# Fused attention, mixture of experts and a last layer on one core: the second pair's bias from SBUF, softplus' sums, gate's and conversion's steps in other places, expert 0's scaling on GpSimd

## The chip, the core and the metric

The kernel runs on one core of a Trainium2 chip. A core has a matrix engine (TensorE), a vector engine (VectorE), a scalar engine (ScalarE, ACT), a general one (GpSimd) and a queue engine (SyncE, SP), each with an instruction stream of its own that runs in order; semaphores tie them together. They work on SBUF, an on-chip memory of 128 partitions; TensorE writes into PSUM, a small memory of eight banks per partition. The metric is the device time of one execution in microseconds.

## What is computed

```python
# attention: q, k, v are (2, 8, 576, 64), s is (2, 8, 576)
scores = q @ k.T / sqrt(64)
cum = cumsum(maximum(s, 0))
scores = where(causal, -1e9, scores + minimum(-(cum[:, None] - cum[None, :]), 0))
x = softmax(scores) @ v                      # -> (1152, 512)
# mixture: w_gate (512, 8), w1 (8, 512, 1024), w2 (8, 1024, 512)
P = exp(x @ w_gate - max)
for _ in range(8):
    P /= P.sum(1, keepdims=True) + 1e-9
    P /= P.sum(0, keepdims=True) + 1e-9
    P *= 1152 / 8
x = sum(P[:, e:e+1] * (maximum(x @ w1[e], 0) @ w2[e]) for e in range(8))
# last layer: w_in (512, 2048) and w_out (2048, 512), given as float64
h = x @ w_in
out = (maximum(h, 0) + log1p(exp(-abs(h)))) @ w_out
```

## The kernel before

All is written under a manual schedule: the order of the Python statements is the order of each engine's instructions, and waits follow from the data.

**Precision.** TensorE multiplies in a reduced float32 type, so every operand is split into a high part (a copy on ACT) and a low part (a subtraction on VectorE or GpSimd), and each product is three matmuls (high x high, low x high, high x low). In names, `xh`, `xl` are the two parts of the activations, `w1h`, `w1l`, `w2h`, `w2l` those of the weights, `hh`, `hl` those of the hidden layer.

**Attention** (until about 121 us) goes over 8 pairs of heads, each in 5 blocks of queries; such a block is a unit. The units are pipelined by hand: in pass n, the letters of "YSKAXVWBTED" do one stage each of different units. The causal bias is brought into the scores as a product of its own: `init_bias` (L436) fills the tiles `bq`, `bk`, `be` of a pair with zeros and ones, and `load_bias` (L444) puts two rows of the cumulative sums per head into them. The sums `cs` lie in SBUF with one row per head (L467 scales s, L469 scans, L474 and L475 split); L477 copies them to DRAM as `c8d`. There are two sets of tiles: set 0 for pair 0 is filled from `cs`, all others from `c8d`. SP issues nearly all transfers in program order: q and k by `load_qk` (L418), the first weights of the mixture, `raw` (L134), bias (L449, L454). GpSimd sums and differences of the first weights (L154, `sums1`) and the scaling of the probabilities by their row sums (L618) stand in one stream. TensorE transposes the probabilities (`tr`, L630) and multiplies them by v (`pv`, L662, L672); ACT copies the transposed ones out of PSUM (`pt`, L650). In the last four pairs of batch 0 and 1, `build` makes the seven combinations of activations that the mixture's products need, one `yield` at a time, two per unit (L82 sums, L85 high, L88 low parts).

**Mixture.** Sixteen half-experts x = 0 to 15 (two per expert, XE = 2). A half-expert's first layer is four quarters of work, done by a scheme of seven products per quarter (`Unit.p1` to `p7`, each six 128x288 matmuls at L286), its second layer is `downs` (three 128x512 matmuls at L371 for each of nine tiles of tokens and four slices of the hidden layer, a yield after each three). `total` adds the finished tile to `acc`: for x < 2 without a gate (L383), then with the factor of the gate (L388), and for x = 2 expert 0's sum is first scaled by its gate (L387). `play` runs strings such as A_SEQ and B_SEQ: a1 to b7 are products, d three matmuls of downs, `=0` to `=2` and `w0` to `w3` put a generator that prepares the next weights in a queue, `back`. After each product or d, `step` moves that queue by one, every sixth time the gate's steps (`gate_steps`, x = 0 and 1), and later every third time the conversion of the last layer's float64 weights to float32 (`convert`, from x = 2; 32 items of seven steps; items come by `fetch`). What an eviction still has to do is put off with `defer(k, ...)` and done k flushes later; products and downs flush once or twice each.

**Switch and last layer.** When x = 15 is done, `turn` transposes the result (L901, L911) back into activations, batch 0 and then 1. The last layer, x = 16 to 19, uses `plain` products (12 matmuls at L350). Its eviction is softplus: three ACT functions (L249 abs, L250 exp, L251 ln), then `sums` (L255 on VectorE, L256 on GpSimd, L257 on VectorE), `high` (L260 VectorE, L261 ACT) and `rest_` (L264 VectorE), over four sets of tiles.

## Time and profile before

| | us |
|---|---|
| runs, median (lowest to highest, 3 runs) | 1129.07 (1127.46 to 1132.74) |
| profiled execution, its own time | 1129.13 |
| its span | 1127.4 |
| TensorE busy | 1085.5 (96%) |
| VectorE busy | 750.0 (67%) |
| ScalarE busy | 525.8 (47%) |
| GpSimd busy | 358.7 (32%) |
| share of the chain that ended last: TensorE / VectorE / ScalarE | 80% / 8% / 5% |

The span is the time from the first to the last instruction in the profile; 1.7 us of the execution lie around it. In a timeline row stand the start, the duration, engine, line, operation and the tile written and read; in brackets how long the engine stood idle before it and what ended that. "x4" are four instructions of one kind in a row. The granted clock is TensorE's, as a share of 2.4 GHz.

### The profile page before, as it was taken

The page shows a single profiled execution, that of the slowest core. Times are in us where ns is not written, and L with a number is a line of the kernel's source. Part 1 is how long each engine was busy: PE and PEld are TensorE (multiplying, and loading weights), DVE is VectorE, ACT ScalarE, POOL GpSimd, SP SyncE. Part 2 cuts the span into 40 slices and gives each one's busy share as a digit, 9 for nine tenths or more (in the row PEclk, how much of TensorE's full clock was granted, in tenths as well). Part 3 has the DMA queues.
Part 4 walks back from the last instruction along what each step waited for, and adds up shares of the span by engine and source line. Part 5 has one row for each costly group of instructions (what it writes and reads, how often), then busy time and mean ns, then how long its engine had stood idle before and what let it go on. Part 6 is the DMA issues. An engine that isn't in the chain of part 4 may idle for free.

```text
span 1127.4 us, 18117 instructions
## 1 busy us (share of the span) xinstructions
PE 1085.5 (96%) x6692; PEld 952.9 (85%) x6692; DVE 750.0 (67%) x1705; ACT 525.8 (47%) x1246; POOL 358.7 (32%) x429
## 2 busy tenths in 40 slices
PE   5989899999999999999999999999999999999998
PEld 4767888797889888888888888988889888888886
DVE  4555537749878787787787777864555576666664
ACT  4988644234334344344343433433334276655552
POOL 8775411112314144141431414322020032323231
PEclk8998999999999999999999999999999999999999
DMA  5222102031322223222232222311112111111002
GB/s 190 71 71 66 39 1 72 4 111 48 113 94 94 94 77 126 88 94 94 94 111 87 94 94 94 103 50 45 38 38 76 38 38 38 38 38 38 1 1 84
DMA packets 30424, 78.48 MB, mean 70 GB/s; under 512 B 6048, under 2 KB 10656, under 8 KB 30336
## 3 DMA queue, kind: packets, MB, share of 16 engines
q1 hardware_dynamic: 27768, 68.93, 18.8%
q0 software_dynamic: 2560, 8.39, 2.0%
q8 instruction: 52, 0.85, 0.3%
q14 instruction: 36, 0.29, 0.1%
q10 hardware_dynamic: 8, 0.01, 0.0%
HBM read 66.02 MB, written 10.82 MB: 68 GB/s over the span
## 4 chain that ended last, share of the span: by engine, by line
PE 80%; DVE 8%; ACT 5%; issue 3%; POOL 3%; DMA 1%; SPq 0%; POOLq 0%; ACTq 0%; DVEq 0%
PE py L371 40%; PE ph L286 30%; PE ph L350 3%; PE sc L550 2%; POOL a L256 1%; DVE a L260 1%; PE pv L662 1%; ACT a L250 1%; ACT a L249 1%; PE tr L636 1%; DVE a L255 1%; ACT eb L605 1%; DVE acc L383 1%; PE tr L630 1%; DVE a L257 1%
## 5 line engine op out<-in xcount | busy, mean ns | idle before, releaser
L371 PE MATMUL py<-w2h,hh 128*128 128x512 f32 x720 | 287.2, 399 | 10.7 <-DVE acc L383 6.3
L371 PE MATMUL py<-w2h,hl 128*128 128x512 f32 x720 | 285.0, 396 | 0.0
L371 PE MATMUL py<-w2l,hh 128*128 128x512 f32 x720 | 284.9, 396 | 0.0
L286 PE MATMUL ph<-xh,w1h 128*128 128x288 f32 x896 | 265.9, 297 | 0.4 <-ACT v L294 0.3
L286 PE MATMUL ph<-xh,w1l 128*128 128x288 f32 x896 | 265.6, 296 | 0.0
L286 PE MATMUL ph<-xl,w1h 128*128 128x288 f32 x896 | 264.2, 295 | 0.0
L286 PEld LDWEIGHTS ph<-xh,w1h 128*128 128x128 f32 x896 | 168.9, 188 | 18.3 <-ACT v L294 1.5
L286 PEld LDWEIGHTS ph<-xl,w1h 128*128 128x128 f32 x896 | 169.2, 189 | 16.6
L286 PEld LDWEIGHTS ph<-xh,w1l 128*128 128x128 f32 x896 | 169.1, 189 | 0.0
L371 PEld LDWEIGHTS py<-w2h,hl 128*128 128x128 f32 x720 | 135.4, 188 | 32.6 <-DVE hl L237 0.2
L371 PEld LDWEIGHTS py<-w2h,hh 128*128 128x128 f32 x720 | 135.4, 188 | 26.6 <-DVE acc L383 8.9
L234 ACT ACTIVATE hh<-ph 128x288 fp32r<-128x288 f32 x192 | 78.4, 410 | 154.7 <-DVE ph L336 85.3
L371 PEld LDWEIGHTS py<-w2l,hh 128*128 128x128 f32 x720 | 135.5, 188 | 11.4
L200 POOL TENSOR_TENSOR w2l<-raw,w2h 128x512 fp32r<-128x512 f32 x40 | 54.1, 1352 | 260.0 <-ACT w2h L198 259.9
L388 DVE SCALAR_TENSOR_TENSOR acc<-py,gate,acc 128x512 f32<-128x512 f32 x126 | 93.8, 745 | 58.2 <-PE py L371 57.2
L294 ACT ACTIVATE v<-ph 128x288 f32<-128x288 f32 x128 | 50.9, 411 | 168.7 <-PE ph L286 160.4
L888 POOL TENSOR_TENSOR cm<-cm,ct 128x512 f32<-128x512 f32 x32 | 45.1, 1409 | 222.4 <-DVE ct L886 222.4
L237 DVE SCALAR_TENSOR_TENSOR hl<-ph,hh 128x288 fp32r<-128x288 f32 x192 | 86.2, 452 | 32.2 <-ACT hh L234 30.1
L256 POOL TENSOR_TENSOR a<-a,a 128x288 f32<-128x288 f32 x64 | 51.8, 809 | 160.1 <-DVE a L255 159.8
L148 DVE TENSOR_TENSOR w1l<-raw,w1h 128x512 fp32r<-128x512 f32 (+1 forms) x144 | 94.3, 655 | 9.8 <-ACT w1h L145 9.5
L145 ACT ACTIVATE w1h<-raw 128x512 fp32r<-128x512 f32 (+1 forms) x144 | 83.0, 576 | 1.6 <-PE ph L286 1.6
L350 PE MATMUL ph<-xh,w1h 128*128 128x288 f32 x256 | 76.0, 297 | 0.8 <-ACT xh L912 0.8
(176 smaller groups left out, 1683.1 us busy)
## 6 DMA issues: line engine op xcount, KB each, us to landing
raw<-in_w SPq DMA_DIRECT2D x64, 512.0 KB
f<-in_w_in SPq DMA_DIRECT2D x16, 512.0 KB
f<-in_w_out SPq DMA_DIRECT2D x16, 512.0 KB
wd<-cm POOLq DMA_DIRECT2D x32, 256.0 KB, 2.6
raw<-wd SPq DMA_DIRECT2D x16, 512.0 KB
out<-acc SPq DMA_DIRECT2D x9, 256.0 KB
vv<-in_v SPq DMA_DIRECT2D x8, 256.0 KB
qk<-in_k SPq DMA_DIRECT2D x7, 288.0 KB
```

The source lines that it names most:

```text
L145: nc.scalar.activation(out=hi[:, o], in_=t[:, src], func=AF.Copy)
L148: nc.vector.tensor_tensor(out=lo[:, o], in0=t[:, src], in1=f(hi[:, o]), op=ALU.subtract)
L200: (nc.gpsimd if i else nc.vector).tensor_tensor(out=lo, in0=t[:, r], in1=f(hi), op=ALU.subtract)
L234: nc.scalar.activation(out=hh, in_=z, func=AF.Relu)
L237: nc.vector.scalar_tensor_tensor(out=hl, in0=z, scalar=0.0, in1=f(hh), op0=ALU.max, op1=ALU.subtract)
L256: nc.gpsimd.tensor_tensor(out=a2, in0=a1, in1=a2, op=ALU.subtract)
L286: nc.tensor.matmul(o, u, v, start=(start and c == 0 and n == 0), stop=(c == 1 and n == 2), skip_group_check=True)
L294: nc.scalar.activation(out=t, in_=self.a, func=AF.Copy)
L350: nc.tensor.matmul(o, u, v, start=(n == 0), stop=(n == 11))
L371: nc.tensor.matmul(py[t], u, v, start=(k == 0 and n == 0), stop=(k == NF - 1 and n == 2))
L388: nc.vector.scalar_tensor_tensor(out=a, in0=py, scalar=gate_t[0][:, t, e:e + 1], in1=a, op0=ALU.mult, op1=ALU.add)
L888: nc.gpsimd.tensor_tensor(out=m, in0=m, in1=f(t), op=ALU.add)
```

## The change

1. **Bias.** `init_bias(1)` runs on VectorE, ahead of the scaling of s; it ran on GpSimd, after the other memsets. The bias of pair 1 comes from `cs` in SBUF and is issued once, behind `split_ends(0)`; it came from `c8d` in DRAM, behind the weights. The write of `c8d` stands behind it.
2. **Build.** Two more yields, that is one unit, between the last sum and `high_(2)`.
3. **Softplus.** `sums` are put off by one flush more, `high` and `rest_` by two; the add of the two sums goes from VectorE to GpSimd.
4. **Expert 0's scaling** goes from `total` on VectorE to the start of a group of downs on GpSimd.
5. **Gate.** A step may come after three (first six steps) or seven others, at least three after an a2 or b2, and not between w0 and the next "=".
6. **Conversion.** Four yields between the first two fetches and the first item.
7. **Switch and end.** The products between downs stand behind them, with one more behind w3 (in the diff the string); the last half's last two tiles are groups of their own.

```diff
--- before.py
+++ after.py
@@ -108,7 +108,8 @@
         sum_(2, nc.gpsimd)
-        yield
+        for _ in range(3):
+            yield
         high_(2)
@@ -253,19 +254,19 @@
             nc.vector.tensor_scalar(a2, a1, 1.0, -1.0, ALU.add, ALU.add)
+            nc.vector.scalar_tensor_tensor(out=a3, in0=z, scalar=0.0, in1=a3, op0=ALU.max, op1=ALU.add)
             nc.gpsimd.tensor_tensor(out=a2, in0=a1, in1=a2, op=ALU.subtract)
-            nc.vector.scalar_tensor_tensor(out=a3, in0=z, scalar=0.0, in1=a3, op0=ALU.max, op1=ALU.add)
+            nc.gpsimd.tensor_tensor(out=a3, in0=a3, in1=a2, op=ALU.add)
...
         def high():
-            nc.vector.tensor_tensor(out=a3, in0=a3, in1=a2, op=ALU.add)
             nc.scalar.activation(out=hh, in_=a3, func=AF.Copy)
...
-        defer(0, sums)
-        defer(2, high)
-        defer(3, rest_)
+        defer(1, sums)
+        defer(4, high)
+        defer(5, rest_)
@@ -362,6 +363,10 @@
                 py[t] = ps.tile([P, DM], F32, tag=f"y{1 + nd[0] % 2}", name="py", bufs=1)
+            if x == XE:
+                for t in tiles:
+                    a = acc[0][:, t, :]
+                    nc.gpsimd.tensor_scalar(a, a, gate_t[0][:, t, 0:1], 1.0, ALU.mult, ALU.mult)
             for k, ft in enumerate((0, 2, 1, 3)):
@@ -383,8 +388,6 @@
             e = x // XE
-            if x == XE:
-                nc.vector.tensor_scalar(a, a, gate_t[0][:, t, 0:1], None, ALU.mult)
             nc.vector.scalar_tensor_tensor(out=a, in0=py, scalar=gate_t[0][:, t, e:e + 1], in1=a,
@@ -433,24 +436,24 @@
-            def init_bias(x):
+            def init_bias(x, engine):
                 for t in (bq_t[x], bk_t[x], be_t[x]):
-                    nc.gpsimd.memset(f(t), 0.0)
+                    engine.memset(f(t), 0.0)
                 for j in range(2):
...
                                          (be_t[x], slice(j * REM, (j + 1) * REM), 1.0)):
-                        nc.gpsimd.memset(f(t[j * D:j * D + 4, cols]), one)
+                        engine.memset(f(t[j * D:j * D + 4, cols]), one)
...
                     h = 2 * p + j
-                    x = c8d[h] if p > 0 else f(cs[h:h + 1])
+                    x = c8d[h] if p > 1 else f(cs[h:h + 1])
                     for t, r, cols in ((bk_t, 2, slice(0, S)), (bq_t, 0, slice(0, S))):
...
                     h = 2 * p + j
-                    x = c8d[h, :, NB * P:] if p > 0 else f(cs[h:h + 1, :, NB * P:])
+                    x = c8d[h, :, NB * P:] if p > 1 else f(cs[h:h + 1, :, NB * P:])
                     nc.sync.dma_start(out=f(be_t[p % BB][j * D:j * D + 2, j * REM:(j + 1) * REM]), in_=x)
@@ -464,17 +467,17 @@
             nc.vector.memset(ones, 1.0)
+            init_bias(1, nc.vector)
             nc.vector.tensor_scalar(s_sb, s_sb, 0.0, 8.0, ALU.max, ALU.mult)
...
                 nc.vector.tensor_tensor_scan(c8[:, a:b], one_row[:, a:b], s_sb[:, a:b], first, ALU.mult, ALU.add)
-            init_bias(0)
+            init_bias(0, nc.gpsimd)
             cs = ac.tile([B * H, 2, S], F32R, name="cs")
...
             load_bias(0)
-            nc.sync.dma_start(out=c8d, in_=f(cs))
             make_identity(nc, ident)
@@ -494,8 +497,6 @@
                 nc.gpsimd.memset(f(y), 0.0)
-            for x in range(1, BB):
-                init_bias(x)
@@ -554,6 +555,8 @@
             split_ends(0)
+            load_bias(1)
+            nc.sync.dma_start(out=c8d, in_=f(cs))
             load_qk(4)
@@ -764,7 +767,8 @@
                     if i == 1 and p + 1 < B * NP:
-                        load_bias(p + 1)
+                        if p > 0:
+                            load_bias(p + 1)
                         load_v(p + 1)
@@ -861,6 +865,8 @@
             fetch(1)
+            for _ in range(4):
+                yield
             for i, (_, dst) in enumerate(todo):
@@ -917,14 +923,20 @@
         back = []
-        tick = [0]
-
-        def step():
+        tick = [0, 0, 0, 0]
+        dense = [False]
+        def step(z=""):
...
             tick[0] += 1
+            tick[1] += 1
+            tick[2] = 0 if z[1:] == "2" else tick[2] + 1
             if x < XE:
-                if tick[0] % 6 == 0:
+                if tick[1] >= (3 if tick[3] < 6 else 7) and tick[2] > 2 and not dense[0]:
                     next(gates, None)
+                    tick[1] = 0
+                    tick[3] += 1
             elif x < NX - 2 and tick[0] % 3 == 0:
@@ -957,6 +969,8 @@
             for z in seq.split():
+                if z[0] in "=w":
+                    dense[0] = z[0] == "w"
                 if z[0] == "=":
@@ -967,7 +981,7 @@
                     todo[z]()
-                step()
+                step(z)
@@ -988,7 +1002,7 @@
             play(A_SEQ if x < NX else A_PLAIN, products(x, 1), downs(x, A_GROUPS))
-            d = downs(x, B_GROUPS)
+            d = downs(x, B_GROUPS if x + 1 < NH else [(t,) for t in range(NB, NTT)])
             if x + 1 < NX:
@@ -1000,7 +1014,7 @@
                 u = products(NX, 0)
-                play("p d d w0 p d d w2 p d d w1 p d d w3", u, d)
+                play("d d w0 p d d w2 p d d w1 p d d w3 p", u, d)
                 back.append(turn(1))
...
```

Line numbers move by one to three in these parts (L449 is now L452, L134 is L135, L249 is L250). How the instructions then stand is shown at three places.

SP, at the start: `bk_94`, `bq_92`, `be_96` are the tiles of set 1, `raw` the first weights. Before, from the write of c8d on:

```order
L477 DMA c8d<-cs 16x1152
L523 DMA endf<-in_q 64x64 x2
L418 DMA qk<-in_k 128x576
L418 DMA qk<-in_q 128x576
L134 DMA raw_181<-in_w 128x1024
L134 DMA raw_183<-in_w 128x1024
L134 DMA raw_185<-in_w 128x1024
L134 DMA raw_187<-in_w 128x1024
L449 DMA bk_94<-c8d 2x576
```

and now, from the third of the four rows for set 1 on:

```order
L452 DMA bk_94<-cs 2x1x576
L452 DMA bq_92<-cs 2x1x576
L457 DMA be_96<-cs 2x1x64 x2
L559 DMA c8d<-cs 16x1152
L421 DMA qk<-in_k 128x576
L421 DMA qk<-in_q 128x576
L135 DMA raw_187<-in_w 128x1024
```

The six pieces for set 1 stand ahead of c8d's write, k, q and the weights; they stood behind all of them.

ScalarE, at the end of attention: `xh_75` are the combinations of batch 1, `pt` the copies of the last but one unit's probabilities. Before:

```order
L85 ACTIVATE xh_75<-xr 128x2x288
L650 ACTIVATE pt<-tr 128x512 x2
L85 ACTIVATE xh_75<-xt 128x4x288
L650 ACTIVATE pt<-tr 128x512
L650 ACTIVATE pt<-tr_1791 64x128
L721 ACTIVATE xr<-pv 128x512
L721 ACTIVATE xr<-pv_1805 128x64
```

and now:

```order
L85 ACTIVATE xh_75<-xr 128x2x288
L653 ACTIVATE pt<-tr 128x512 x3
L653 ACTIVATE pt<-tr_1791 64x128
L85 ACTIVATE xh_75<-xt 128x4x288
L724 ACTIVATE xr<-pv 128x512
L724 ACTIVATE xr<-pv_1805 128x64
L85 ACTIVATE xh_75<-xr 128x288
```

The copy of the combined tile xt stands behind the last copies of pt instead of between them.

ScalarE, in the last layer (L249 to L251 are the three functions, L261 the high part; the number of `a` tells the product apart). Before:

```order
L249 ACTIVATE a_10585<-ph 128x288
L250 ACTIVATE a_10585<-a_10585 128x288
L251 ACTIVATE a_10587<-a_10585 128x288
L261 ACTIVATE hh<-a_10587 128x288
L249 ACTIVATE a_10618<-ph 128x288
L250 ACTIVATE a_10618<-a_10618 128x288
L251 ACTIVATE a_10620<-a_10618 128x288
```

and now (L250 to L252 and L262):

```order
L250 ACTIVATE a_10583<-ph 128x288
L251 ACTIVATE a_10583<-a_10583 128x288
L252 ACTIVATE a_10585<-a_10583 128x288
L262 ACTIVATE hh<-a_10554 128x288
L250 ACTIVATE a_10616<-ph 128x288
L251 ACTIVATE a_10616<-a_10616 128x288
L252 ACTIVATE a_10618<-a_10616 128x288
L262 ACTIVATE hh<-a_10585 128x288
```

L261 stood right behind its own product's functions; L262 stands behind those of the next product.

## Rows read from the trace of the kernel before

**Rows 1.** Page, part 1: busy time, share of the span and instructions of each engine.

```profile
PE 1085.5 (96%) x6692; PEld 952.9 (85%) x6692; DVE 750.0 (67%) x1705; ACT 525.8 (47%) x1246; POOL 358.7 (32%) x429
```

**Rows 2.** Windows: us of stretch, busy per engine, granted clock, DMA share.

```profile
122.00:125.40 3.40, 3.40 (x17) 3.28 (x18) 3.15 (x6) 2.15 (x4) 0.81 (x1) 0.50 0.00 0
200.50:203.90 3.40, 3.40 (x13) 2.90 (x12) 2.10 (x9) 0.77 (x2) 0.90 (x2) 0.50 0.02 5
339.00:386.50 47.50, 47.50 (x278) 42.58 (x277) 37.84 (x74) 18.73 (x43) 15.34 (x16) 1.00 0.28 95
912.00:926.00 14.00, 12.17 (x87) 10.78 (x85) 12.43 (x27) 11.90 (x29) 5.32 (x6) 1.00 0.23 77
977.00:1024.50 47.50, 45.73 (x270) 40.74 (x269) 31.70 (x71) 27.75 (x66) 13.43 (x16) 1.00 0.15 45
```

**Rows 3.** TensorE's waits: awaited instruction; us in total, times, longest.

```profile
PE py L371 <- DVE acc L383: 6.3, 6, 1.5
...
PE py L371 <- DVE acc L388: 3.4, 2, 2.5
PE pcs L830 <- DVE hl L237: 3.1, 1, 3.1
PE sc L550 <- DMA bq<-cs: 2.8, 1, 2.8
PE pv L672 <- ACT pt L650: 1.9, 1, 1.9
```

**Rows 4.** SP's timeline, start: start, us, issue, pieces [idle before <-releaser].

```profile
7.49 1.21 SPq L454 DMA_DIRECT2D be<-cs  x2
...
11.65 1.85 SPq L134 DMA_DIRECT2D raw<-in_w  x4
```

**Rows 5.** VectorE's timeline, start of the kernel.

```profile
0.91 0.54 DVE L464 MEMSET one_row<- 16x576 f32 x1 [0.91 <-PEq L1049]
...
2.54 0.77 DVE L467 TENSOR_SCALAR s_sb<-s_sb 16x576 f32<-16x576 f32 x1 [0.95 <-DMA s_sb<-in_s]
```

**Rows 6.** Timelines of GpSimd, then TensorE, pair 0, units 0 and 1.

```profile
17.07 0.73 POOL L154 TENSOR_TENSOR raw<-raw 128x256 f32<-128x256 f32 x1 [1.64 <-DMA raw<-in_w]
17.77 0.94 POOL L618 TENSOR_SCALAR eb<-eb,st 128x256 f32<-128x256 f32 x2
...
20.15 0.82 PE L550 MATMUL sc<-bk,bq 64*128 64x128 f32 x2 [3.91 <-DMA bq<-c8d]
20.90 1.11 PE L630 MATMUL tr<-ident,eb 128*128 128x128 f32 x4
```

**Rows 7.** ScalarE's timeline, end of attention.

```profile
119.58 1.16 ACT L85 ACTIVATE xh<-xt 128x1152 fp32r<-128x1152 f32 x1 [1.97 <-POOL xt L82]
```

**Rows 8.** VectorE's timeline in the gate, x = 1.

```profile
195.11 0.23 DVE L837 TENSOR_REDUCE gs<-gate 128x9 f32<-128x72 f32 x1
...
197.31 0.45 DVE L237 SCALAR_TENSOR_TENSOR hl<-ph,hh 128x288 fp32r<-128x288 f32 x1
```

**Rows 9.** VectorE's timeline, first item of the conversion.

```profile
253.65 0.43 DVE L870 TENSOR_SCALAR f<-f 128x512 f32<-128x512 f32 x1 [5.96 <-DMA f<-in_w_in]
```

**Rows 10.** The chain that ended last, in the last layer: start, us, what.

```profile
1002.98 0.93 PE py L371 x4
1003.91 1.59 PE ph L350 x12
...
1008.65 0.40 ACT a L249
...
1010.01 0.82 POOL a L256
1010.85 0.47 DVE a L260
...
1011.69 0.41 ACT a L249
```

**Rows 11.** VectorE's timeline, switch, second set of transposes.

```profile
919.58 0.98 DVE L264 TENSOR_TENSOR hl<-a,hh 128x288 fp32r<-128x288 f32 x1
```

## The prediction

> **What bounds the kernel now.** I began with the page. TensorE is busy for 96% of the span [rows 1], so at most some 42 us are open, and its own matmuls are not changed. Then a table of windows: a whole steady half-expert has TensorE busy for 47.50 of 47.50 us [rows 2], and in the listing of TensorE's waits no large entry falls there. So work that the change moves in the steady part is worth nothing; what can move lies in stages where TensorE idles: the start of attention, its end, the gate, the start of the conversion, the switch and the last layer. The waits [rows 3] name them. Last I read, for each, the engine TensorE waited for and what stood ahead of the awaited instruction there. The windows also show what an idle stretch costs behind itself: after the gate's long wait and after the end of attention the granted clock is 0.50 (the lower level, 1.2 GHz) for 3.40 us each [rows 2], about 1.7 us of lost work each time.
>
> The profiled execution took 1129.13 us, its span is 1127.4 us, and the median of the runs is 1129.07; the sum is made against 1129.13, so against the median as well.
>
> **Start: the second pair's bias.** Nine memsets go to VectorE ahead of the scaling of s. Six have 576 columns; the one of that length took 0.54 us, and with three short ones that is about 3.5 us. VectorE sat idle there for 0.95 us until s had landed at 2.54 [rows 5]. It was free at about 1.6 (the memset at 0.91 and a short one), so it gets to the scaling near 5.0 instead of 2.54: 2.5 us later. No other work hides that: TensorE's first scores wait 2.8 us for this very bias [rows 3]. All of pair 0 moves by 2.5.
> SP then issues the second bias from SBUF (six pieces, 0.6 us each by the pair that took 1.21: 3.6 us) ahead of the four weight loads, which so far began at 11.65 [rows 4]. Now they begin near 11.65 + 2.5 + 3.6 = 17.75. The first weight's sum on GpSimd started 17.07, that is 5.4 us after the first issue, after a wait of 1.64 us for the load [rows 6]; it would start at about 23.2. In GpSimd's order it stands ahead of the scaling of unit 1, whose transposes TensorE started at 20.90. Sum 0.73 plus half of the scaling's 0.94: the transposes start near 24.4, so 3.5 us later. What goes is the wait of 3.91 us for the bias [rows 6]: the bias itself lands near 16.7, before TensorE asks for it at about 18.2. So a wait for the weights takes the place of the wait for the bias. The loads have less beside them now and may land sooner, so I take **-3.0**. GpSimd loses the nine memsets, and c8d's write moves behind the second bias; the first to need either is the third pair's bias, many units later, so both count nothing. Its ends: -5, when the memsets and GpSimd's collide as well, and +1.4, when the weights are in time.
>
> **End of attention: the build is two units later.** ACT's conversion of xt waited 1.97 us for GpSimd's sum and then took 1.16 [rows 7]; the copies of pt stand behind it, and TensorE waited 1.90 for those [rows 3]. Afterwards the copies stand ahead of it. The gain is not 1.9, since the last quick build follows on ACT and limits TensorE's third product next: with half clock granted there anyway [rows 2], that product comes 1.7 us earlier by my count. I take **+1.7** (0.5 to 3.4, the upper end with the half clock gone). In the middle of attention the same sums slow GpSimd and VectorE beside it; **+0.5** (-1 to +3).
>
> **Gate.** Each step of the normalisation is a chain on VectorE: from 195.11 seven small operations ran to 197.3, and the eviction hl stood behind them [rows 8]. TensorE waited 3.1 us for such an hl [rows 3] and lost 1.7 by the clock behind that [rows 2]. Smaller gaps at six places from 140 to 215 us add some 2.5 by the starts of the matmuls. That is 7.3 us. The new rule keeps the steps out of the stretch that begins with w0, where VectorE also makes w2's low parts, and runs the first six steps sooner, so that all still fit in the same two half-experts. VectorE remains full in the first part of x=1, where three or four steps now fall; I leave 1.3 us of waits there: **+6.0** (3.5 to 7.5).
>
> **Conversion's start and expert 0's scaling.** VectorE stood still for 5.96 us until the first item landed, its first step being in its queue already [rows 9]; behind it queued evictions and the totals, and TensorE waited 3.4 us in two places for L388 [rows 3]. Four more yields put the first step 12 play steps (some 9 us at this pace) behind the fetch, longer than the landing took. Nine scalings leave VectorE too; on GpSimd they start with their group. One of 512 columns costs there at most 512/288 of the 0.81 us that L256 takes [rows 10], 1.4 us, and four steps of the group, over 2 us of matmuls, lie ahead of the total that reads it. So I cost them at nothing; were GpSimd late, each of nine totals would wait up to 1 us. The gaps of this stage are 4.7 us with restarts and small ones; I leave 0.7: **+4.0** (2.5 to 5).
>
> **Switch.** From 912 to 926 us TensorE is busy 12.17 of 14 [rows 2], since products and transposes alternate faster than ACT and VectorE serve them. Two more products behind the last transpose, and the deferral, spread this. I take **+1.2** (0 to 2.5).
>
> **Last layer: softplus' ring.** This is the part the change touches most. In the chain, ACT's first function of a product (1008.65) is followed by steps on ACT and VectorE, GpSimd's L256 (0.82 us at 1010.01), VectorE's L260 (1010.85), ACT's L261, and only then by the next product's first function at 1011.69 [rows 10]: one turn of the ring is 3.04 us. TensorE needs 12 matmuls, 1.59 us, and six of the downs at 0.93/4 each [rows 10], 2.99 in all, so the ring is a little slower, and the totals that stand behind it on VectorE come late: TensorE waits for L383 six times, 6.3 us [rows 3], with restarts and one wait for ACT's first total about 7.7. After the change ACT reaches L261 two or three flushes after its input is due, so the turn no longer closes through GpSimd. GpSimd has 2 x 0.82 = 1.64 us of work in each 2.99. The split of the last pair into single groups takes away one of the six waits.
> A price stands against that. VectorE's L264 (both operands in SBUF) took 0.98 us beside GpSimd in the switch [rows 11], while L260, of the same form, took 0.47 alone [rows 10]; so GpSimd's second add can hold VectorE up. VectorE is busy for 31.70 of 47.5 us [rows 2], 2.00 a product; without L260 1.53. If nothing meets, the gain is 7.7. If every microsecond of the adds stopped it, 1.53 + 1.64 = 3.17 against 2.99: 64 products x 0.18 = 11.5 lost, against 7.7. I take **+6.0** (-4 to 8), near the upper end, because in the turn of rows 10 L256 ran beside L257 alone, which reads PSUM and took no longer for it.
> The Trainium skill, page "SBUF — State Buffer", section "SBUF: two separate sides", says that VectorE and GpSimd share one port pair under an exclusive lock, so that the later of two such operations stands still for the whole of the other. Rows 11 agree for L264. By it every VectorE operation of this form that meets the two adds would wait for their ends, and the term would be -4; without it 7.7.
>
> **The sum.** -3.0 + 1.7 + 0.5 + 6.0 + 4.0 + 1.2 + 6.0 = 16.4 us. 1129.13 - 16.4 = 1112.7; I say 1112 us, since the gaps left over were each rounded up.
>
> **Rivals.**
> 1. *The weights are in time at the start.* For it: only 1.64 us of wait before, and the bias's transfers no longer lie beside theirs. Against it: SP issues them 6 us later [rows 4]. Then unit 1 starts near 19.5 rather than 20.90; +1.4 and not -3.0, with less idle time before the half clock: about 1107. Chance 0.12.
> 2. *The last layer keeps its waits.* VectorE, held up by the adds, reaches L383 as late as before. For it: rows 11. Against it: nothing waits for the adds within two flushes any more. The 6 us stay: 1118. Chance 0.15.
> 3. *The gate's steps still hold up evictions* in x=1, as they come closer together at first. For it: each is over 2 us of VectorE [rows 8]; against: from the seventh on, six other play steps lie between two of them. About 5 us stay: 1117. Chance 0.10.
> 4. *Slower: GpSimd becomes a lock on VectorE in all of the last layer.* If both adds of each product stop it for their whole length, and half of the 1.0 us per product that it now idles (15.8 of 47.5 us [rows 2]) stays, its product costs 1.53 + 1.64 + 0.5 = 3.67 us. It decides from 2.99 on: 64 products x 0.68 = 43.5 us, and the 6 us aren't gained: 1161. For it: rows 11; against: L256 met L264 only in the switch, and the deferral lets VectorE fill its idle time. Chance 0.03. The skill's lock, named above, is the rule that would bring this about.
> 5. *All terms at their low ends.* -5 + 0.5 - 1 + 3.5 + 2.5 + 0 - 4 = -3.5: about 1132.6. The order moves, but other instructions keep the engines late. Chance 0.05.
>
> **How the numbers follow.** The forecast has the remaining 0.55; its own spread, from the ends of single terms taken apart, is some 7 us either way. The range 1102 to 1122 takes in the forecast's spread, rivals 1, 2 and 3, and leaves out 4, 5 and a share of the forecast's tails, about 2 in 10. A measurement of this kernel can tell about 0.5%, 5.6 us, from no change: faster means below 1123.5, slower above 1134.7. Forecast and rivals 1 to 3 are faster nearly throughout (0.92, less 0.02 of tails), rival 5 is the same, rival 4 slower.
>
> **What would show it.** Start: the scaling of s near 5.0, the first weight load near 17.6, unit 1's transposes near 24, waiting by way of GpSimd for a weight and not for bq. Gate: no pcs or pg wait over 1 us and no half clock near 200. Conversion: VectorE not idle for 6 us near 247, no L388 wait over 1 us. Last layer: turns of about 2.99, L383 waits under 2 us in all, ACT not waiting for VectorE before L261. Wrong would be: a wait for bq as before, L264 or L255 in the last layer beyond 0.8 us on average with TensorE waiting, or half-experts in the steady part longer than 47.5 us.

## The result

The changed kernel takes 1119.48 us in the median of four runs (1118.16 to 1121.51), the kernel before 1128.91 in the same comparison; the ratio is 0.9915 with a 95% interval of 0.9895 to 0.9935. That is 9.6 us less by the ratio and 9.4 by the medians, where 17 were predicted: inside the range, and little more than half of the forecast gain. The profiled execution took 1118.75 us, its span is 1117.0.

The page of the changed kernel, first busy time and share of each engine, as in [rows 1]:

```profile
PE 1080.4 (97%) x6692; PEld 951.8 (85%) x6692; DVE 737.8 (66%) x1641; ACT 528.1 (47%) x1246; POOL 419.6 (38%) x493
```

TensorE's waits in the changed kernel, to be held against [rows 3] (awaited instruction; us in total, times, longest):

```profile
PE py L376 <- DVE acc L388: 6.1, 3, 2.1
PE tr L633 <- POOL eb L621: 5.7, 2, 5.5
PE sc L551 <- DMA bq<-cs: 5.6, 1, 5.6
...
PE ph L287 <- ACT v L295: 2.5, 1, 2.5
...
PE py L376 <- ACT acc L385: 1.0, 1, 1.0
PE py L376 <- DVE hl L238: 1.0, 1, 1.0
```

Gone are the waits for bq from DRAM (3.9 us), for L388 of before (3.4; the line is L391 now), for pcs (3.1) and the one for pt ahead of L672 (1.9). New are 5.7 us for GpSimd's L621 and 2.5 for ACT's v, and the first scores' wait for their bias from `cs` has grown from 2.8 to 5.6 us, as the later scaling of s made it. And the one that the largest term counted on losing is still there: L388, which was L383, with 6.1 us instead of 6.3.

Marks along TensorE's order, read from the starts of its matmuls in the two traces, tell where each stage stands. The mark of a half-expert is the first matmul of its downs; the last row ends with the end of the last matmul.

| stretch | before | after | difference | predicted |
|---|---|---|---|---|
| start to the first pv | 23.09 | 26.47 | +3.4 | +3.0 |
| from there to the downs of x = 0 (rest of attention, first products) | 118.88 | 115.44 | -3.4 | -2.2 |
| x = 0 to x = 2 (gate) | 106.64 | 100.34 | -6.3 | -6.0 |
| x = 2 to x = 4 (start of the conversion) | 100.09 | 94.96 | -5.1 | -4.0 |
| x = 4 to x = 15 | 522.28 | 522.28 | 0.0 | 0 |
| x = 15 to x = 16 (switch) | 57.07 | 55.05 | -2.0 | -1.2 |
| x = 16 to the last matmul | 195.19 | 198.35 | **+3.2** | **-6.0** |

Five stretches came out within 1.2 us of their terms, and the steady part has not moved at all. One went the other way, by 9 us.

Three of the differences are those of one execution each. In the kernels of the experiments below that have the changed kernel's order in a stretch, the first pv comes at 25.6 to 27.3 us, the rest of attention takes 115.4 to 119.4 us and the last layer 196.5 to 200.0. The gate (100.3 us), the conversion's start (94.96) and the steady part (522.28) are alike in all of them to some hundredths.

**The start** went by the steps of the prediction. From the timelines of VectorE, SP, GpSimd and TensorE in the changed kernel, to be read beside [rows 4 to 6]:

```profile
5.65 0.45 DVE L471 TENSOR_SCALAR s_sb<-s_sb 16x576 f32<-16x576 f32 x1
...
18.01 1.85 SPq L135 DMA_DIRECT2D raw<-in_w  x4
...
23.01 0.72 POOL L155 TENSOR_TENSOR raw<-raw 128x256 f32<-128x256 f32 x1 [5.32 <-DMA raw<-in_w]
23.71 0.94 POOL L621 TENSOR_SCALAR eb<-eb,st 128x256 f32<-128x256 f32 x2
...
24.25 1.15 PE L633 MATMUL tr<-ident,eb 128*128 128x128 f32 x4 [5.48 <-POOL eb L621]
```

The scaling of s starts at 5.65 us (predicted 5.0), the first weight's issue at 18.01 (17.75), GpSimd's sum at 23.01 (23.2), after 5.32 us of waiting for that weight, and unit 1's transposes at 24.25 (24.4). The wait for bq from DRAM is gone, and a longer one for a weight that has nothing to do with attention has taken its place, because GpSimd's sum stands ahead of the scaling.

**The last layer.** The chain that ended last, in the changed kernel, up to TensorE's first wait for L388 (start, us on the chain, what):

```profile
970.71 0.46 ACT hh L262
...
971.19 0.57 DVE hl L265
971.76 0.85 DVE a L256
...
972.74 0.82 POOL a L258
...
973.62 0.91 POOL a L259
...
974.56 0.02 ACT hh L262
...
975.34 0.45 ACT a L251
...
975.81 0.32 DVE a L256
...
977.94 0.45 ACT hh L262
...
978.41 0.04 DVE hl L265
...
979.46 0.61 DVE acc L388
...
980.11 0.96 PE py L376 x3
```

VectorE's L265 (high minus low) of a product stands ahead of L256 of a later one; GpSimd's L258 needs that L256, L259 follows L258, and ACT's L262 waits for L259. From there the chain goes on in ACT's order, where L250 and L251 of another product stand behind L262, to the next L256, and over GpSimd once more. The last L265 waited for L262; behind it on VectorE stand L256 and L257 of another product, and only then L388, for which TensorE waited 1.97 us. From one L262 to the next it is 3.85 us and then 3.38; the turn of before, in [rows 10], was 3.04. So the ring through ACT's order has not gone, and VectorE's order has come into it: L265, which waits for ACT, stands ahead of L256, which feeds the ring, and ahead of the total. The same lines lead to the second wait. The three waits are some 2 us each, and behind the second and third the clock falls, as the windows show (stretch, busy times, the third number from the end is the granted clock):

```profile
1033.00:1037.00 4.00, 3.97 (x14) 3.50 (x15) 3.35 (x6) 1.85 (x5) 2.56 (x3) 0.57 0.02 4
1087.40:1091.50 4.10, 3.99 (x14) 3.53 (x15) 1.70 (x5) 1.34 (x4) 2.42 (x4) 0.58 0.34 128
```

By these two rows 1.7 us of clock are missing in each (0.43 of 4.00 us, 0.42 of 4.10), 3.4 together. That is the whole of the stage's 3.2 us: its waits for totals are 7.1 us (6.1 for L388 and 1.0 for L385), against 7.0 before (6.3, and 0.7 for the same copy on ACT), where no half clock followed. The kernels below that have the same order in this stage agree: 196.5 us with one such stretch of half clock, 198.0 to 198.4 with two, 199.8 and 200.0 with three.

### The profile page after: what moved, and what is told of

It reads as the page before. It is cut to its first block, busy times and chain, and to the rows that moved or that the text cites. A ratio compares the mean times of both kernels' runs of the same rounds, so it can differ in the third digit from the quotient of the medians.

```text
span 1117.0 us, 18144 instructions
## 1 busy us (share of the span) xinstructions
PE 1080.4 (97%) x6692; PEld 951.8 (85%) x6692; DVE 737.8 (66%) x1641; ACT 528.1 (47%) x1246; POOL 419.6 (38%) x493
## 4 chain that ended last, share of the span: by engine, by line
PE 82%; DVE 7%; ACT 5%; POOL 3%; issue 2%; SPq 1%; DMA 0%; POOLq 0%; DVEq 0%; ACTq 0%
PE py L376 41%; PE ph L287 31%; PE ph L351 4%; POOL a L259 2%; PE sc L551 1%; POOL a L258 1%; PE pv L665 1%; DVE a L256 1%; DVE hl L265 1%; PE tr L639 1%; ACT hh L262 1%; ACT a L251 1%; ACT eb L608 1%; PE tr L633 1%; ACT a L250 1%
## 5 line engine op out<-in xcount | busy, mean ns | idle before, releaser
L287 PE MATMUL ph<-xh,w1h 128*128 128x288 f32 x896 | 265.1, 296 | 2.5 <-ACT v L295 2.5
L391 DVE SCALAR_TENSOR_TENSOR acc<-py,gate,acc 128x512 f32<-128x512 f32 x126 | 94.0, 746 | 54.2 <-PE py L376 54.0
L238 DVE SCALAR_TENSOR_TENSOR hl<-ph,hh 128x288 fp32r<-128x288 f32 x192 | 86.7, 454 | 30.5 <-ACT hh L235 28.7
L149 DVE TENSOR_TENSOR w1l<-raw,w1h 128x512 fp32r<-128x512 f32 (+1 forms) x144 | 99.8, 694 | 8.3 <-ACT w1h L146 8.2
L265 DVE TENSOR_TENSOR hl<-a,hh 128x288 fp32r<-128x288 f32 x64 | 38.0, 594 | 71.9 <-ACT hh L262 71.9
L258 POOL TENSOR_TENSOR a<-a,a 128x288 f32<-128x288 f32 x64 | 51.8, 809 | 78.8 <-DVE a L256 61.4
```

The costliest lines, as they stand in the source:

```text
L149: nc.vector.tensor_tensor(out=lo[:, o], in0=t[:, src], in1=f(hi[:, o]), op=ALU.subtract)
L238: nc.vector.scalar_tensor_tensor(out=hl, in0=z, scalar=0.0, in1=f(hh), op0=ALU.max, op1=ALU.subtract)
L258: nc.gpsimd.tensor_tensor(out=a2, in0=a1, in1=a2, op=ALU.subtract)
L265: nc.vector.tensor_tensor(out=hl, in0=a3, in1=f(hh), op=ALU.subtract)
L287: nc.tensor.matmul(o, u, v, start=(start and c == 0 and n == 0), stop=(c == 1 and n == 2), skip_group_check=True)
L391: nc.vector.scalar_tensor_tensor(out=a, in0=py, scalar=gate_t[0][:, t, e:e + 1], in1=a, op0=ALU.mult, op1=ALU.add)
```

## Experiments

All times are medians; a ratio is taken against runs of the kernel before on the same chip, and the changed kernel's own ratio is 0.9915.

### What bounds the last layer

**L265 later.** One number in the changed kernel.

```diff
-        defer(5, rest_)
+        defer(6, rest_)
```

> The changed kernel with one number changed: softplus' low part (L265) is put off by six flushes, not five, so that VectorE does the next product's L256 and L257 before it. Theory (a new ring): in the changed kernel L265 of a product stands on VectorE ahead of L256 of the next, waits for ACT's L262, which waits for GpSimd's second add, which waits for L256 of its own product: one turn of 3.4 us against TensorE's 2.99. With the order turned round a turn covers two products, so the three waits for L388 (6.1 us), the two half-clock stretches behind them and the wait for ACT's total go: 7 to 9 us less, about 1111 us. Rival (GpSimd's 1.62 us per product and its lock on VectorE's port): GpSimd does the same work, so at most 2 us less, and L388 waits of over 4 us remain.

1112.52 us, ratio 0.9855 (0.9840 to 0.9870): 7.0 us less. TensorE's waits for L388 in this kernel:

```profile
PE py L376 <- DVE acc L388: 1.5, 3, 0.5
```

and VectorE's timeline at the same place as above:

```profile
977.19 0.31 DVE L256 TENSOR_SCALAR a<-a 128x288 f32<-128x288 f32 x1 [0.32 <-ACT a L251]
977.67 0.46 DVE L257 SCALAR_TENSOR_TENSOR a<-ph,a 128x288 f32<-128x288 f32 x1 [0.17 <-ACT a L252]
978.44 0.31 DVE L256 TENSOR_SCALAR a<-a 128x288 f32<-128x288 f32 x1 [0.32 <-ACT a L251]
978.92 0.46 DVE L257 SCALAR_TENSOR_TENSOR a<-ph,a 128x288 f32<-128x288 f32 x1 [0.17 <-ACT a L252]
979.93 0.57 DVE L265 TENSOR_TENSOR hl<-a,hh 128x288 fp32r<-128x288 f32 x1 [0.56 <-ACT hh L262]
```

L256 and L257 of two products now stand ahead of the L265 that waits for ACT. The rest of the wait is 1.5 us, no half clock follows it, and from x = 16 to the last matmul the kernel takes 189.51 us: 5.7 less than the kernel before and 8.8 less than the changed one. GpSimd does the same 128 operations as in the changed kernel. The chain up to the first wait runs along TensorE until 976.28 in this kernel, and from there over one product's L250 and L251 on ACT and its L256 to L265. So the order on VectorE made the wait, and not GpSimd's load.

**The add back on VectorE.**

```diff
-            nc.gpsimd.tensor_tensor(out=a3, in0=a3, in1=a2, op=ALU.add)
         def high():
+            nc.vector.tensor_tensor(out=a3, in0=a3, in1=a2, op=ALU.add)
             nc.scalar.activation(out=hh, in_=a3, func=AF.Copy)
```

> The changed kernel with the add of softplus' two sums back on VectorE (ahead of L262), everything else, the later flushes too, as changed. Ring theory: the turn loses one of its two GpSimd adds (0.81 us) for one of 0.46 on VectorE, 3.4 - 0.35 = 3.05 or a little less, close to TensorE's 2.99: most of the waits go, 4 to 8 us less than the changed kernel, 1112 to 1115 us. Rival (GpSimd's load and lock): the gain is the same 6 to 8 us, and here, other than with L265 later alone, L265 and L256 have no long ones (over 0.8 us).

1127.13 us, ratio 0.9975 (0.9959 to 0.9990): 7.6 us *more* than the changed kernel. Both expectations missed. TensorE's waits for L388:

```profile
PE py L376 <- DVE acc L388: 7.8, 3, 2.7
```

and three lines of VectorE's timeline ahead of the first of them:

```profile
969.58 1.54 DVE L261 TENSOR_TENSOR a<-a,a 128x288 f32<-128x288 f32 x1 [0.64 <-POOL a L258]
...
973.75 0.98 DVE L261 TENSOR_TENSOR a<-a,a 128x288 f32<-128x288 f32 x1
...
976.20 1.01 DVE L261 TENSOR_TENSOR a<-a,a 128x288 f32<-128x288 f32 x1
```

L261, the add, now stands on VectorE behind L257 and ahead of L265. There it waits itself for GpSimd's L258 (0.64 us idle), and beside GpSimd's operations it takes 1.54, 0.98 and 1.01 us; its median is 0.46. All three lie on the chain that leads to the first wait. I had taken 0.35 us off the turn for an add that is faster on VectorE, and had counted neither the wait nor the longer time. In this profile three stretches of half clock fall into the last layer, one more than in the changed kernel's. From x = 18's downs to x = 19's this kernel needs 55.04 us for 16 products, 3.44 each, the changed kernel 54.48 (3.41), the kernel before 53.85 (3.37) and the one with L265 later 51.35 (3.21).

**Both at once.** The add on VectorE, L265 put off by six flushes.

> The changed kernel with L265 put off by six flushes and the add back on VectorE: the first of these alone took 7.0 us off, the second alone added 7.6. If only the order on VectorE matters (the ring), this is as fast as with L265 later alone, 1112 to 1114 us. If the add itself is dear where it stands on VectorE (it waits there for GpSimd and blocks what follows), it stays above 1117.

1114.30 us, ratio 0.9862 (0.9841 to 0.9883), just above the expected span and by the times not to be told from L265 later alone (0.9855). The trace has it slower in its stage: 191.8 us from x = 16 to the last matmul instead of 189.5, with 3.6 us of waits for L388. So with the order turned round it makes little or no difference which engine adds; with the order of the changed kernel it makes 7.6 us. The order counts for most of it.

**Softplus as before.** The change's third part undone: flushes 0, 2 and 3, the add on VectorE.

> The changed kernel with the whole softplus part undone (flushes 0, 2 and 3, the add on VectorE). If the changed kernel's last layer is no better than that of before, as its trace reads (TensorE's waits there 7.1 us with 2 us of half clock behind two of them, against 7.0 before), this takes the same time within 2 us, 1117.5 to 1121; the prediction's step would have had it 6 us longer, 1125.

1116.94 us, ratio 0.9898 (0.9881 to 0.9915): 2.5 us less than the changed kernel, a little below the expected span. From x = 16 to the last matmul it takes 195.21 us, the time of the kernel before (195.19) within 0.03 us. So in these profiles this part of the change costs 3.1 us in its stage, which is the half clock above; by the times it costs 1.9 to 2.5, and the intervals of the two ratios overlap. The single groups at the end, which are in this kernel, leave five waits for L388 (5.8 us) instead of six (6.3), and no gain in the stage's time.

### The start

**The bias as before.** The change's first part undone.

> The changed kernel with the bias part undone: memsets of set 1 on GpSimd, c8d written at once, pair 1's bias from DRAM behind the weights. The prediction's step: the part costs 3.0 us; its trace shows unit 1's transposes at 24.25 instead of 20.90. So 3 us less, about 1116.3 us. Rival: the later start is taken back in the middle of attention, where the same units stand beside other work, and the time is the same within 1 us.

1115.40 us, ratio 0.9883 (0.9868 to 0.9899): 4.1 us less by the medians, 3.6 by the ratios. The step held: this part costs 3 to 4 us. TensorE waits as it did before, for bq from DRAM, but 4.9 us instead of 3.9.

**The weights' preparation two units later.**

```diff
-                if n >= 3:
+                if n >= 5:
                     next(prework, None)
```

> The changed kernel with the first weights' preparation (the sums L155, L157 on GpSimd and what follows) begun in pass 5 instead of 3, so that it stands behind the scaling of units 1 and 2. Theory: in the changed kernel TensorE's wait of 5.5 us at 24.2 is GpSimd's sum waiting for a weight that SP issues only at 18.0; with the sum out of the way unit 1's transposes start near 18.7 instead of 24.25, as soon as the scaling's own input is there, and the half clock behind the wait (24 to 31 us) goes: 5 to 7 us less, about 1113.5. Rival: the second bias itself is what comes late: then TensorE waits for bq <- cs there and the gain is under 2 us.

1116.33 us, ratio 0.9875 (0.9860 to 0.9889): 3.2 us less by the medians, 4.5 by the ratios, since this chip's runs of before are 1.3 us longer. That is less than the 5 to 7 expected. The timelines of TensorE around unit 1 and of GpSimd's sum:

```profile
20.05 0.31 PE L551 MATMUL sc<-bk,bq 64*128 64x128 f32 x2
20.30 0.66 PE L633 MATMUL tr<-ident,eb 128*128 128x128 f32 x4
...
24.84 0.73 POOL L155 TENSOR_TENSOR raw<-raw 128x256 f32<-128x256 f32 x1 [3.21 <-DVE st L619]
```

The window from 24 to 31 us in this kernel, and then in the changed one (the granted clock is the third number from the end):

```profile
24.00:31.00 7.00, 5.08 (x47) 3.74 (x47) 2.70 (x12) 5.00 (x15) 6.16 (x7) 1.00 0.87 280
```

```profile
24.00:31.00 7.00, 6.75 (x43) 4.95 (x44) 1.81 (x10) 4.48 (x13) 7.00 (x11) 0.61 0.83 272
```

Unit 1's transposes start at 20.30 (18.7 expected) without a wait, so the second bias was there in time; GpSimd's sum runs behind the scaling of unit 2. The clock is 1.00 there, where it was 0.61 in the changed kernel. The start's whole gain is 4.9 us (first pv at 21.55 instead of 26.47). In the profiled execution, the longest of the four, all but 1.0 us of it is given back by the downs of x = 0; by the times 3 to 4.5 us stay.

**The memsets behind the split of the sums.** They stay on VectorE.

> The changed kernel with the nine memsets of set 1 still on VectorE, but behind the split of the cumulative sums. By the prediction's step the first bias is 2.5 us earlier again, SP issues all that follows 2.5 us earlier (weights near 15.5), and the wait for GpSimd's sum ends 2.5 us earlier as well: 2.5 us less, about 1117. Rival: VectorE's first maxima of unit 0 now stand behind the memsets and take the gain back: under 1 us.

1117.36 us, ratio 0.9889 (0.9875 to 0.9903): 2.9 us less by the ratios, 2.1 by the medians. The first pv is 2.2 us earlier (24.23), and the wait for GpSimd's L621 is as long as in the changed kernel (5.3 us). The cost of the memsets was as predicted, and unit 0's maxima did not take it back.

### The other parts

**The build as before.** One yield instead of three.

> The changed kernel with the build's two extra yields taken out. The prediction's step has it 1.7 us better at the end of attention and 0.5 in the middle. The trace of the changed kernel reads otherwise: TensorE begins the mixture without a pause, but then waits 2.5 us for ACT's v, since the last build's chain is bound by ACT and VectorE. Expected: 1 to 2 us longer, 1120.5 to 1121.5, with a pause at pv and half clock behind it as before. Rival: the two extra yields also take 2.6 us out of the middle, so 3 to 4 us longer.

1123.12 us, ratio 0.9935 (0.9922 to 0.9949): 2.3 us more by the ratios, 3.6 by the medians, and the intervals touch. The pause at pv is back (2.2 us). The half clock that was expected behind it is not: the granted clock is 1.00 from 126 to 145 us. In the middle the picture isn't clear: from the 61st pv matmul to the downs of x = 0 the profile of this kernel shows 106.8 us, the changed kernel's 102.7, but the profiles of seven other experiments, which have the changed kernel's order there, lie between 102.6 and 106.3 us (four of them at 102.6 or 102.7). At both ends of that the order is the same; what differs is the clock, as below. What the build's part is worth lies between nothing and 4 us, and stays open within that.

At the end of attention the changed kernel shows why the part brought less there than the wait it took away, in the timelines of ACT, VectorE, and ACT and TensorE again:

```profile
120.48 1.17 ACT L85 ACTIVATE xh<-xt 128x1152 fp32r<-128x1152 f32 x1 [0.77 <-POOL xt L82]
...
121.68 1.36 DVE L88 TENSOR_TENSOR xl<-xt,xh 128x1152 fp32r<-128x1152 f32 x1 [3.52 <-ACT xh L85]
...
123.64 1.37 DVE L82 TENSOR_TENSOR xt<-xr,xt 128x288 f32<-128x288 f32 x2
...
125.10 1.17 ACT L85 ACTIVATE xh<-xt 128x1152 fp32r<-128x1152 f32 x1 [1.95 <-DVE xt L82]
126.17 0.39 ACT L295 ACTIVATE v<-ph 128x288 f32<-128x288 f32 x1
...
126.62 0.40 PE L287 MATMUL ph<-xh,w1h 128*128 128x288 f32 x1 [2.52 <-ACT v L295]
```

The low part L88 of the late xt (1.36 us on VectorE at 121.68) now stands ahead of the last build's sums L82; ACT's L85 waits 1.95 us for those, the copy of v stands behind it, and TensorE waits 2.52 for v. It starts the third product at 126.62, against 126.95 before.

**Expert 0's scaling on VectorE.**

> The changed kernel with expert 0's scaling back on VectorE in front of L391. The prediction costed the scaling on GpSimd at nothing and gave the whole of the conversion's term to the items' later start. If so, this costs 0 to 1.5 us (nine operations of about 0.5 us on VectorE, one or two waits of 0.3 to 0.5 by TensorE); all nine on the path would be 4.5 us.

1118.68 us, ratio 0.9911 (0.9889 to 0.9933): no difference. In its stage (x = 2 to x = 4) it takes 95.79 us, 0.8 more than the changed kernel. Costed at nothing, rightly.

**The gate as before**, every sixth step.

```diff
-                if tick[1] >= (3 if tick[3] < 6 else 7) and tick[2] > 2 and not dense[0]:
+                if tick[0] % 6 == 0:
```

> The changed kernel with the gate's steps taken at every sixth play step again. The stretch from x=0's first downs to x=2's was 106.6 us before and is 100.3 in the changed kernel. If that is the gate's rule alone: 6 us longer, about 1125.5, with TensorE waiting over 2.5 us for an hl that stands behind a gate step and half clock behind it. Rival: the later start of the stretch, not the rule, moved the steps against the evictions: under 3 us.

1125.22 us, ratio 0.9961 (0.9946 to 0.9976): 5.2 us more by the ratios, 5.7 by the medians. TensorE's waits show the two old ones:

```profile
PE pcs L834 <- DVE hl L238: 3.1, 1, 3.1
...
PE pg L811 <- DVE hl L238: 1.0, 1, 1.0
```

In the trace the stretch from x = 0 to x = 2 is 107.93 us, 7.6 longer than in the changed kernel. The gate's term stands.

**The conversion's first item at once**, without the four yields.

> The changed kernel without the four yields ahead of the conversion's first item. If the late start of the items is what the stage gained by, VectorE stands still for about 6 us near 240 and TensorE waits 2 to 3 us behind: 3 to 4.5 us longer, about 1123. If expert 0's scaling on GpSimd does part of it, under 3.

1121.52 us, ratio 0.9927 (0.9905 to 0.9949). By the times this isn't settled: 1.4 us by the ratios, runs from 1118.6 to 1125.3. The profiled execution, the longest of them, shows the mechanism. VectorE's timeline and TensorE's wait:

```profile
248.66 0.43 DVE L874 TENSOR_SCALAR f<-f 128x512 f32<-128x512 f32 x1 [7.18 <-DMA f<-in_w_in]
```

```profile
PE py L376 <- DVE acc L391: 3.1, 1, 3.1
```

The stretch from x = 2 to x = 4 is 99.89 us, 4.9 longer than the changed kernel's. So in that execution the yields were worth nearly the whole term; in others the item may have landed sooner.

**Three repairs at once.** L265 by six flushes, the weights from pass 5, the memsets behind the split.

> The changed kernel with L265 put off by six flushes, the weights' preparation from pass 5 and the memsets behind the split of the sums, all at once. If the three causes lie in different stages, their gains add: -7.0 for the ring, -5 to -7 and -2.5 at the start, which overlap (without the weights' wait the start is bound by the bias alone): 1119.5 - 7 - 7 to 9 = 1103.5 to 1106. If the start's gain is taken back later in attention: about 1110.

1105.25 us, ratio 0.9781 (0.9766 to 0.9796): the fastest of all, 25.0 us under the runs of before beside it and 1.3% under the changed kernel. TensorE is busy for 98% of its span:

```profile
PE 1081.1 (98%) x6692; PEld 951.7 (86%) x6692; DVE 745.3 (67%) x1641; ACT 527.6 (48%) x1246; POOL 419.2 (38%) x493
```

The first pv is at 18.42 us (26.47 in the changed kernel), x = 16 to the last matmul 189.52. So the start gains 8.0 us and the last layer 8.8; attention gives back 3.7 of it, at a mean granted clock of 0.93 between the first pv and x = 0 where the changed kernel had 0.97, and the span is 12.8 us shorter than the changed kernel's.

## Why the prediction was right, and where it failed

**The bound.** Only stages in which TensorE idled moved; x = 4 to 15 took 522.28 us in both kernels. This step held to the hundredth.

**Start: held**, in sign, size and mechanism: +3.4 against +3.0, and 3.6 to 4.1 when undone. The working by queues (so many issues ahead of the weights, the sum ahead of the scaling) gave each time within 0.7 us. Rival 1, weights in time, is out.

**End of attention and build: mechanism half right.** The end was sized at 1.7 with ACT and VectorE next in line; the half clock there did go in this execution, and the wait for v took most of that back. That it went is chance: five of the kernels above (L265 later, the weights two units later, the memsets behind the split, the gate as before, the three repairs) have the new order there too, and 3.4 us of half clock between 121 and 132 us. The middle gave more than 0.5 in this profile, but that isn't to be told from the scatter.

**Gate and conversion: held**, -6.3 for -6.0 and -5.1 for -4.0. Undone, the gate is worth 5 to 6 us in the times; the conversion's share is shown in a trace alone. Rival 3 is out: the steps in x = 1 left one wait of 1.0 us for L238.

**Switch: held**, -2.0 for -1.2. With softplus undone it is still 55.48 us against 57.07, so most of it comes from the products put behind the transposes; no run undoes these alone.

**Last layer: wrong by 9 us, and here is the whole miss.** The step that failed is the sentence that after the change "the turn no longer closes through GpSimd". I had looked at ACT's order, in which L262 indeed stands one product later, and not at VectorE's. `rest_` put off by five flushes and a later product's `sums` put off by one fall into the same flush wherever two downs follow a product, and the older comes first: L265 of a product, then L256 of a later one, and the total behind both. So what leads to TensorE's waits still closes through GpSimd, by L256, L258, L259 and L262, and from L262 on through VectorE's order (L265) or ACT's (L250, L251), at 3.85 and 3.38 us a turn. The waits stayed as long as they were (7.1 us against 7.0), which is the 6 us not gained, and two of them drew the half clock behind them, which is the 3 us lost on top. The 6.0 us were the right size for a ring really broken: with L265 one flush later the stage gains 5.7 over the kernel before.
The period that I held against the ring was also too narrow. I took 2.99 us for a product with two downs; a half of the last layer has 36 downs to 16 products, by [rows 10] 16 x 1.59 + 36 x 0.70 = 50.6 us or 3.16 a product. The stage with the totals in it ran at 3.37 before.

So rival 2 is what happened: the last layer keeps its waits, and its price (6 us, 1118) is close to the measured time. That the price fits is in part chance, since two stretches of half clock are in the measured time that it did not count, and other profiles of the same order have one or three. And its reason was another one. It blamed the adds for holding VectorE up, and the runs deny that this makes the waits: with two adds on GpSimd and L265 later the kernel is as fast as with one. Rival 4, the lock, is out with it. What the lock does can be seen in durations (shortest, median, longest in ns) of L256, L265 and L259 in the changed kernel, and last of L265 in the kernel with L265 later:

```profile
L256 DVE TENSOR_SCALAR a<-a x64: 298/304/920, 895.5 to 1099.0; 128x288 f32<-128x288 f32 x64
...
L265 DVE TENSOR_TENSOR hl<-a,hh x64: 443/459/1072, 900.3 to 1101.6; 128x288 fp32r<-128x288 f32 x64
...
L259 POOL TENSOR_TENSOR a<-a,a x64: 799/812/1209, 898.7 to 1100.3; 128x288 f32<-128x288 f32 x64
...
L265 DVE TENSOR_TENSOR hl<-a,hh x64: 446/664/1123, 903.5 to 1095.3; 128x288 fp32r<-128x288 f32 x64
```

The changed kernel's medians are those of the undisturbed operation (304, 459 and 812 ns). The longest L256 and L265 take two to three times as long, and L259 took 1209 ns where VectorE's L149 ran beside it. The rule of the Trainium skill (page "SBUF — State Buffer", section "SBUF: two separate sides"), that of two such operations on VectorE and GpSimd one stands still for the other, agrees with the longest of L265 and L259. They are not rare: 16 of the 64 L265 and 14 of the 64 L256 take over 0.8 us, and one of these L256 lies on the chain shown above (0.85 us). But in the kernel with L265 later the median L265 takes 664 ns, so it is held up more often there, and that kernel is 7 us faster: there the time lost is off TensorE's path. By the rule alone the term would have been a loss of 4 us; the measured effect of a second add on GpSimd, with the order turned round, is nothing that can be measured in the times (0.9855 against 0.9862).

The total came out inside the range because the start, the gate and the conversion were costed rightly and the range left room for the last layer's waits, not because that layer was understood.

## What to carry to other kernels

When work is put off to break a ring, write down, for every engine of the ring, in which order the put-off pieces of neighbouring rounds now stand, not only for the engine that was seen waiting. Two pieces that fall into the same flush are a new ring if the older one waits for another engine and the younger one feeds it; putting one of them off by a single flush more was worth 7 us here. To find such a ring, read the chain that leads to a wait. And when a load is moved ahead of others on a queue, follow what is now late to the engine that waits for it in order: a preparation with time to spare stood in front of work that had none.

## What was not expected of the hardware

Executions of the same order of instructions differ by some 4 us in attention alone, and the granted clock shows it. From 80 to 104 us in the changed kernel and then in the kernel with L265 later, which differ only in the last layer (windows, the granted clock third from the end):

```profile
80.00:104.00 24.00, 22.50 (x236) 17.16 (x234) 15.44 (x69) 21.84 (x61) 19.15 (x26) 0.99 0.16 49
```

```profile
80.00:104.00 24.00, 23.10 (x204) 17.46 (x200) 14.17 (x63) 20.36 (x56) 17.57 (x23) 0.84 0.15 43
```

In the one the clock stays at 0.99, in the other it is 0.84, though both programs are the same up to the switch. The kernel before had 0.86 there. So a term of a microsecond or two in that stretch can't be read from one profile of each kernel. The last layer shows it too, where the same order of instructions had one, two or three stretches of half clock behind its three waits of about 2 us.
